# An attention and expert kernel: its attention loop with all five engines in the written order, routing in pieces, and weight casts on GpSimd

## The chip, the core and the metric

The kernel runs on one core of a Trainium2 chip. A core has five engines with a queue of instructions each: TensorE (PE, matrix products), VectorE (DVE), ScalarE (ACT), GpSimd (POOL) and SyncE (SP, which here issues DMAs). They wait for one another through semaphores. The metric is the device time of one execution in microseconds (us), and lower is better.

## The reference

Eight batches of twelve heads go through a sigmoid attention; the result is the input of a layer of eight experts, of which each token takes one. Cut to what matters:

```
scores = (q @ k^T) / sqrt(64) - log(448)          # 8 batches, 12 heads, 448 x 448
x      = (1 / (1 + exp(-scores))) @ v              # as 3584 tokens x 768
logits = normalise(x) @ normalise(expert_emb).T / tau
expert = argmax(logits);  gate = softmax(logits)[expert]
out[token] = gate * (relu(x @ w1[expert]) @ w2[expert])   # w1 768x1024, w2 1024x768
```

Weights, q and k are float32. The kernel makes of each a high half in 16 bits and a low half (value minus high half) in 16 bits, so that three products of 16-bit halves stand for one in float32.

## The kernel before, in words

**The attention loop** runs over 48 pairs of heads. In a pair TensorE makes three blocks of scores (`scores(i, 0..2)`, L364), and the fourth, shorter one for the next pair (`scores_tail(i + 1)`, L377); it turns the packed q and k of pair i + 2 (`turn`, L334) and multiplies the sigmoids with v (`av`, L392). ScalarE makes the sigmoids (L366, and L379 for the tail). `split` makes the halves of q and k out of what was turned: on VectorE for the first head (L344, L345), on ScalarE and VectorE for the second (L342, L345). `evac` brings the result of `av` out of PSUM: the high half on ScalarE (L406) and the low half on VectorE (L408). GpSimd packs q and k of pair i + 3 (`pack`, L323).

**The buffers that tie the engines together.** The pool `ps_s` has three PSUM tiles, and a pair takes four: three blocks of scores and the result of `av`. So the third block of pair i + 1 goes where the result of pair i lay, and has to wait for its `evac`. The pool `ps_t` has one tile: what is turned for pair i + 2 and the scores' tail of pair i + 1 use it in turn, so the tail waits for the `split`.

**Work beside it.** Six pairs make a batch, and two batches a group of 896 tokens. In the pairs behind a batch `chunk` computes router products (L415, summed on VectorE at L417) and `rows` turns the tokens' rows by DMA, stores them (L429, L432) and adds and squares them for the norm (GpSimd L436, ScalarE L442). Behind each of the first three groups, `route1` picks each token's expert (VectorE, L461 to L468), and `route2` counts with TensorE (L475, L476) and works out each token's place (L480 to L488, of which the last is seven comparisons into the tile POH). `select`, `early1` and `early2` do the same for an expert and two blocks of tokens that start early. From pair 30 on the weights of that expert and of the next come in by SyncE (`fetch`, L168), one piece of 128 rows in a pair, into four staging tiles; VectorE casts the high half (`high_v`, L176) and the low half (`low`, L180).

**What sets the order.** In the loop SyncE and TensorE run in the order in which the code is written (`tc.manual_schedule`). For ScalarE, VectorE and GpSimd a scheduler places the instructions by its own model of time; `tc.issue_after` sets a lower limit for a few of them. The routing's steps stand in a pair behind `scores_tail` and ahead of `evac`. Behind the loop come the rest of the router, then the experts' two layers, block of tokens by block of tokens.

## Time and profile before

| | us |
|---|---|
| median of 3 runs (892.04 to 898.67) | 892.21 |
| the profiled execution | 892.36 |
| its span, from the first instruction to the last | 890.6 |
| TensorE busy in the span | 808.4 |
| VectorE, ScalarE, GpSimd busy | 395.7, 392.8, 216.8 |
| the attention loop, first score product to last product with v | 14.4 to 360.4 |

The profile gives each group of instructions by line, engine and operation, with busy time, mean duration and the idle time of the engine ahead of it. A wait is put down to the instruction that ended it. L numbers are lines of the kernel before; the listing of the changed kernel has lines of its own (L345 there is L350, L408 is L411, L468 is L470, L364 is L367, L377 is L380, L392 is L395).

### The profile page before, as it was taken

What the parts mean: (1) busy time and instruction counts of PE and PEld (TensorE: products, weight loads), DVE (VectorE), ACT (ScalarE), POOL (GpSimd) and SP (SyncE); (2) the same over time, 40 slices, a digit from 0 to 9 for tenths busy, and PEclk for the clock granted to TensorE, in tenths of its full rate; (3) what the DMA queues carried; (4) which work ended last, traced back from release to release, by engine and by line L of the source; (5) the groups of instructions that cost most, each with busy time, mean ns of one, the idle gap of its engine ahead of it and who ended that gap; (6) DMA issues with size and microseconds to landing.
All of it is one profiled execution on the core that took longest, in us unless ns stands there. A gap on an engine that the chain in (4) does not pass through costs nothing. (4 is left out here: it accounts for less than half of the span.)

```text
span 890.6 us, 17187 instructions
## 1 busy us (share of the span) xinstructions
PE 808.4 (91%) x5720; PEld 395.0 (44%) x5720; DVE 395.7 (44%) x727; ACT 392.8 (44%) x610; POOL 216.8 (24%) x260
## 2 busy tenths in 40 slices
PE   5999989998998789898859999799999999999794
PEld 2444434343434343354425555345555555555452
DVE  4444454355577663776234115742521012434740
ACT  5667676765675666133233114542421012424540
POOL 2122333242233240113202122122121213130211
PEclk9999999999999999999969999989999999999988
DMA  5665767482989594767999569999997549779973
GB/s 145 172 151 158 170 178 168 140 216 81 244 264 263 159 227 133 169 134 198 205 198 230 135 122 288 286 250 233 294 154 127 126 104 245 217 158 275 276 215 46
DMA packets 252601, 168.13 MB, mean 189 GB/s; under 512 B 192412, under 2 KB 229766, under 8 KB 252464
## 3 DMA queue, kind: packets, MB, share of 16 engines
q1 hardware_dynamic: 242272, 131.13, 63.4%
q0 software_dynamic: 9200, 35.03, 13.4%
q8 instruction: 69, 1.13, 0.5%
q14 instruction: 68, 0.56, 0.2%
q10 hardware_dynamic: 992, 0.29, 0.1%
HBM read 103.02 MB, written 23.99 MB: 143 GB/s over the span
## 5 line engine op out<-in xcount | busy, mean ns | idle before, releaser
L219 PE MATMUL pss<-w,xt 128*128 128x512 f16 x900 | 198.5, 379 | 2.1 <-DVE hr L252 1.1
L231 PEld LDWEIGHTS <-hT 128*128 128x128 f16 x1296 | 129.5, 101 | 123.6 <-SPq L915 16.2
L231 PE MATMUL pss<-w,hT 128*128 128x384 f16 x768 | 138.1, 343 | 28.3 <-SPq L915 15.3
L366 ACT ACTIVATE att<-pss,bias_s 128x896 f32<-128x896 f32 x144 | 135.5, 1012 | 3.9 <-PE pss L364 2.9
L219 PEld LDWEIGHTS <-xt 128*128 128x128 f16 x900 | 87.5, 98 | 106.9 <-issue 4.4
L392 PE MATMUL pss<-att,vt 128*64 128x448 f32 x576 | 125.3, 560 | 8.5 <-ACT att L366 4.3
L954 POOL DMA_INDIRECT out<-ob,six x64 | 70.0, 1094 | 210.9 <-ACTq L915 124.1
L250 ACT ACTIVATE hr<-pss 128x512 f16<-128x512 f32 x66 | 37.0, 595 | 180.9 <-PE pss L219 127.0
L364 PE MATMUL pss<-kq 64*128 64x448 f16 x864 | 101.4, 356 | 12.1 <-DVE xT L408 7.2
L252 DVE SCALAR_TENSOR_TENSOR hr<-pss,hr 128x512 f16<-128x512 f32 x66 | 43.5, 687 | 150.8 <-ACT hr L250 143.3
L231 PE MATMUL pso<-w,hT 128*128 128x384 f16 x528 | 87.6, 326 | 0.0
L180 DVE SCALAR_TENSOR_TENSOR w<-stage_w,w 128x768 f16<-128x768 f32 (+1 forms) x78 | 75.9, 1002 | 22.0 <-ACT w L172 19.7
L345 DVE SCALAR_TENSOR_TENSOR kq<-ptr,kq 128x512 f16<-128x512 f32 x96 | 63.0, 657 | 45.5 <-ACT kq L342 43.8
L172 ACT ACTIVATE w<-stage_w 128x768 f16<-128x768 f32 (+1 forms) x78 | 66.5, 877 | 34.2 <-DMA stage_w<-in_moe_w 28.3
L323 POOL COPY pk<-qk 128x384 f32<-128x384 f32 x94 | 48.9, 547 | 122.3 <-issue 83.6
L924 POOL DMA_INDIRECT xg<-xs,gix x31 | 33.1, 1066 | 182.9 <-DMA xt<-xg 141.5
L392 PEld LDWEIGHTS pss<-att,vt 128*64 128x64 f32 x576 | 34.5, 136 | 80.7 <-ACT att L366 51.5
L180 DVE SCALAR_TENSOR_TENSOR w<-stage,w 128x1024 f16<-128x1024 f32 (+1 forms) x48 | 57.8, 1229 | 15.5 <-ACT w L172 14.9
L364 PEld LDWEIGHTS <-kq 64*128 64x128 f16 x864 | 38.9, 95 | 47.2 <-issue 16.5
L408 DVE SCALAR_TENSOR_TENSOR xT<-pss,xT 128x384 f16<-128x384 f32 x96 | 33.0, 384 | 53.2 <-ACT xT L406 27.0
L379 ACT ACTIVATE att_t<-ptr,bias_s 128x448 f32<-128x448 f32 x47 | 29.8, 634 | 55.6 <-PE ptr L377 42.1
L436 POOL TENSOR_TENSOR xf<-xrow 128x768 f32<-128x768 f16 x24 | 39.5, 1644 | 21.2 <-ACT xq L442 18.8
(197 smaller groups left out, 640.4 us busy)
## 6 DMA issues: line engine op xcount, KB each, us to landing
stage_w<-in_moe_w SPq DMA_DIRECT2D x64, 384.0 KB, 4.7
stage<-in_moe_w SPq DMA_DIRECT2D x40, 512.0 KB, 4.8
qk<-in_q SPq DMA_DIRECT2D x48, 192.0 KB, 3.8
qk<-in_k SPq DMA_DIRECT2D x48, 192.0 KB, 3.6
vt<-in_v SPq DMA_DIRECT2D x48, 192.0 KB, 3.4
xs<-xrow POOLq DMA_DIRECT2D x24, 384.0 KB, 4.1
stage_w<-in_moe_w SPq DMA_DIRECT2D x14, 512.0 KB, 4.5
stage<-in_moe_w SPq DMA_DIRECT2D x8, 384.0 KB, 4.2
```

The source lines that it names most:

```text
L172: nc.scalar.activation(wts[st][i][:, c, :], s, AF.Copy, scale=SW)
L180: nc.vector.scalar_tensor_tensor(wts[st][i + 1][:, c, :], s, SW, wts[st][i][:, c, :], op0=ALU.mult, op1=ALU.subtract)
L219: nc.tensor.matmul(ph[half][:, t % 2], xt[:, xi, kc, :], wts[st][wi][:, kc, half * HF:(half + 1) * HF], start=(n == 0), stop=(n == len(L1_ ...
L231: nc.tensor.matmul(po[d][:, :HD], hs[fc // 4][:, i, fc % 4, :], wts[st][wi][:, fc, d * HD:(d + 1) * HD], start=(n == 0), stop=(n == len(L2 ...
L252: d = nc.vector.scalar_tensor_tensor(hr[:, 1], ps, 0.0, hr[:, 0], op0=ALU.max, op1=ALU.subtract)
L323: en.tensor_copy(t.rearrange("p c h d -> p h c d"), qk[i][:, j])
L345: last_split[0] = nc.vector.scalar_tensor_tensor(lo[:, :n, h], x, SQK, hi[:, :n, h], op0=ALU.mult, op1=ALU.subtract)
L364: nc.tensor.matmul(ps[:, h, :S], x[r, ki, c * P:(c + 1) * P], x[r, qi, QC], start=(n == 0), stop=(n == 2))
L366: sig[0] = nc.scalar.activation(a, ps[:, :, :S], AF.Sigmoid, bias=bias_s, scale=1.0 / (8.0 * SQK * SQK))
L392: nc.tensor.matmul(pav[i][h * D:(h + 1) * D, :S], w, m, start=(c == 0), stop=(c == CM))
L436: nrm[1].tensor_tensor(xf, xr[:, 0], xr[:, 1], op=ALU.add)
L954: ins = mark[ET.Pool] = nc.gpsimd.indirect_dma_start(out.rearrange("n (h d) -> (n h) d", h=2), bass.IndirectOffsetOnAxis(ap=six[:, d, c:c ...
```

## The change

- In the loop ScalarE, VectorE and GpSimd are under the written order too, and the code of a pair is put in a new sequence: loads, `pack` of pair i + 3, scores 0 and 1, turning of pair i + 2, scores 2, `split`, squares, stores and adds of rows, turning of rows, routing pieces, low weight casts of the pair before, high weight cast and fetch of the next piece, `av`, the tasks behind a batch, `evac`, and last the tail of the scores.
- In a pair that has a square, `split` has both its high halves on VectorE (`busy`).
- `route1` runs a pair later, from the list `fill`, in the pair whose `route2` stands behind `av`; the rest of `route2` (new function `ranks`), of `select` (`choose`) and of `early1` (`early_tokens`) runs a pair later.
- High weight casts are on GpSimd, and the low cast of a piece comes a pair after its high cast. Two pieces at most are under way instead of four.

```diff
         def high_v():
             for c, s in zip(chunks, tiles):
-                nc.vector.tensor_scalar(wts[st][i][:, c, :], s, SW, None, op0=ALU.mult)
+                nc.gpsimd.tensor_scalar(wts[st][i][:, c, :], s, SW, None, op0=ALU.mult)
...
-        return ((ET.SP, fetch), (ET.DVE, high_v) if vec else (ET.Activation, high), (ET.DVE, low))
+        return ((ET.SP, fetch), (ET.Pool, high_v) if vec else (ET.Activation, high), (ET.DVE, low))
...
-        def split(ps, i):
+        def split(ps, i, busy=False):
...
-                if h:
+                if h and not busy:
                     nc.scalar.activation(hi[:, :n, h], x, AF.Copy, scale=SQK)
                 else:
                     nc.vector.tensor_scalar(hi[:, :n, h], x, SQK, None, op0=ALU.mult)
...
                 xq = nrm[0].tile([P, DM], mybir.dt.bfloat16, name="xq")
-                with tc.issue_after(sig[0].ins):
-                    nc.scalar.activation(xq, xf, AF.Square, accum_out=N2[:, g * JG + j:g * JG + j + 1])
+                nc.scalar.activation(xq, xf, AF.Square, accum_out=N2[:, g * JG + j:g * JG + j + 1])
...
             nc.vector.tensor_reduce(RK[:, sl], t2, axis=AX.X, op=ALU.add)
+
+            def rest():
+                ranks(g)
+
+            if g < NG - 1:
+                fill.append(rest)
+            else:
+                rest()
+            return pst[:, JG * E:JG * E + E]
+
+        def ranks(g):
+            j0 = g * JG
+            sl = slice(j0, j0 + JG)
             if g > GE:
                 member(sl, JG)
...
-            r = [[lambda: chunk(g, 3, 4)], [lambda: chunk(g, 5, 6)],
-                 [lambda: route1(g)], [lambda: route2(g)]]
+            r = [[lambda: chunk(g, 3, 4)], [lambda: chunk(g, 5, 6), lambda: fill.append(lambda: route1(g))],
+                 [lambda: route2(g)]]
...
-        with tc.manual_schedule(engines={ET.SP, ET.PE}):
+        lows = []
+        with tc.manual_schedule(engines={ET.SP, ET.PE, ET.Activation, ET.DVE, ET.Pool}):
             for i in range(NPAIR):
...
-                now[0] = i
-                if i in lag:
-                    lag.pop(i)()
-                if rowq:
-                    rows(*rowq.pop(0))
+                if i + 3 < NPAIR:
+                    pack(i + 3, 1)
+                    pack(i + 3, 0)
+                sq, norms[:] = norms[:], []
                 scores(i, 0)
                 scores(i, 1)
                 if i + 2 < NPAIR:
-                    turns(i + 2)
-                task()
+                    ps = ps_t.tile([P, 2, 512], F32, tag="tr", name="ptr")
+                    for j in (1, 0):
+                        turn(ps, i + 2, j)
                 scores(i, 2)
-                task()
+                if i + 2 < NPAIR:
+                    split(ps, i + 2, bool(sq))
+                for f in sq:
+                    f()
+                old, lag[:] = lag[:], []
+                for f in old:
+                    f()
+                if rowq:
+                    rows(*rowq.pop(0))
+                fs, fill[:] = fill[:], []
+                for f in fs:
+                    f()
+                for f in lows:
+                    f()
+                lows[:] = []
+                if er:
+                    if wp and (wts[1][0] is not None or wp[0][0] == 0):
+                        _, hi, lo = wp.pop(0)[1]
+                        hi[1]()
+                        lows.append(lo[1])
+                    if wq and len(wp) < 2:
+                        fetch_next()
                 for c in range(CM + 1):
                     av(i, c)
-                if i + 1 < NPAIR:
-                    scores_tail(i + 1)
...
                 evac(i)
-                if i + 3 < NPAIR:
-                    pack(i + 3, 1)
-                    pack(i + 3, 0)
-                task()
+                if i + 1 < NPAIR:
+                    scores_tail(i + 1)
```

Three places show what this does to the order of the instructions. First VectorE where the first group is routed: in the kernel before, pair 15 and the start of pair 16 (kq is the split of q and k, t, RK, KT, PM and POH belong to `route2`, xT is the `evac`):

```order
L344 TENSOR_SCALAR kq<-ptr 128x8x64
L345 SCALAR_TENSOR_TENSOR kq<-ptr,kq 128x8x64
L345 SCALAR_TENSOR_TENSOR kq<-ptr,kq 128x7x64
L480 TENSOR_TENSOR t_1631<-pss,OH 128x56
L481 TENSOR_REDUCE RK<-t_1631 128x7
L575 TENSOR_SCALAR KT<-RK 128x7
L576 TENSOR_SCALAR KT<-KT 128x7
L486 SCALAR_TENSOR_TENSOR PM<-KT,RK 128x7
L488 TENSOR_SCALAR POH<-iota_82,PM 128x128 x7
L408 SCALAR_TENSOR_TENSOR xT<-pss,xT 128x3x128
L408 SCALAR_TENSOR_TENSOR xT<-pss,xT 128x64
```

And now, pair 14, from behind its `split` on (L, MX, t, m, OH and CUM belong to `route1`):

```order
L463 TENSOR_SCALAR L<-L,rtau 128x56
L464 TENSOR_REDUCE MX<-L 128x7
L465 TENSOR_TENSOR t_1516<-L,MX 128x56
L466 TENSOR_TENSOR t_1516<-t_1516,cst 128x56
L467 TENSOR_REDUCE m_1517<-t_1516 128x7
L468 TENSOR_TENSOR OH<-t_1516,m_1517 128x56
L470 TENSOR_TENSOR CUM<-CUM,OH 128x8 x7
L482 TENSOR_TENSOR t_1542<-pss,OH 128x56
L483 TENSOR_REDUCE RK<-t_1542 128x7
L411 SCALAR_TENSOR_TENSOR xT<-pss,xT 128x3x128
L411 SCALAR_TENSOR_TENSOR xT<-pss,xT 128x64
```

The seven comparisons into POH no longer stand between two halves of `route2` and an `evac`; they come in the next pair, behind its `split`. All of `route1` now stands between the `split` and the part of `route2` that reads TensorE's counts, within one pair.

Second, TensorE at the same routing: before, at the end of pair 15 (ptr<-kq is the tail of the scores, OH and CUM are what `route1` wrote, the last row begins pair 16):

```order
L377 LDWEIGHTS kq
L377 MATMUL ptr<-kq 128x448
L475 LDWEIGHTS upper_80
L475 MATMUL pss<-OH,upper_80 128x56
L476 LDWEIGHTS ones_81
L476 MATMUL pss<-CUM,ones_81 128x56
L364 LDWEIGHTS kq
L364 MATMUL pss<-kq 128x448
```

Now, at the end of pair 14:

```order
L395 MATMUL pss<-att,vt 64x448 x6
L395 MATMUL pss<-att_t,tv_129 64x448 x2
L477 LDWEIGHTS upper_80
L477 MATMUL pss<-OH,upper_80 128x56
L478 LDWEIGHTS ones_81
L478 MATMUL pss<-CUM,ones_81 128x56
L380 LDWEIGHTS kq
L380 MATMUL ptr<-kq 128x448
```

The two products of `route2` stand ahead of the tail of the scores, in the same pair in which VectorE makes OH and CUM.

Third, VectorE in a pair with a weight cast (w_0_73 is the high half, w_1_74 the low half, L417 belongs to a `chunk`); before:

```order
L176 TENSOR_SCALAR w_0_73<-stage 128x1024
L180 SCALAR_TENSOR_TENSOR w_1_74<-stage,w_0_73 128x1024
L344 TENSOR_SCALAR kq<-ptr 128x8x64
L345 SCALAR_TENSOR_TENSOR kq<-ptr,kq 128x8x64
L345 SCALAR_TENSOR_TENSOR kq<-ptr,kq 128x7x64
L417 TENSOR_REDUCE L<-pss 128x16
L408 SCALAR_TENSOR_TENSOR xT<-pss,xT 128x3x128
L408 SCALAR_TENSOR_TENSOR xT<-pss,xT 128x64
```

Now:

```order
L349 TENSOR_SCALAR kq<-ptr 128x8x64
L350 SCALAR_TENSOR_TENSOR kq<-ptr,kq 128x8x64
L349 TENSOR_SCALAR kq<-ptr 128x7x64
L350 SCALAR_TENSOR_TENSOR kq<-ptr,kq 128x7x64
L180 SCALAR_TENSOR_TENSOR w_1_74<-stage,w_0_73 128x1024
L411 SCALAR_TENSOR_TENSOR xT<-pss,xT 128x3x128
L411 SCALAR_TENSOR_TENSOR xT<-pss,xT 128x64
```

The cast no longer stands ahead of the `split`, its high half has left VectorE, and in this pair, which has a square, the `split` has four instructions there instead of three.

More of the change, by code (lines that the diff above doesn't have):

```diff
@@ L446, in first @@
                 xf = add()
-                lag[now[0] + 1] = lambda: square(xf)
+                norms.append(lambda: square(xf))
             if now[0] < NPAIR:
-                lag[now[0] + 1] = first if now[0] + 1 not in lag else (lambda f=lag[now[0] + 1]: (f(), first()))
+                lag.append(first)
             else:
@@ L663, in attn_moe_kernel @@
                 if i == 0:
[L664 to L670 removed]
+                    expert_prep()
         now[0] = NPAIR
         ended.append(1)
[L673 to L676 removed]
+        for fs in (lag, norms, lows):
+            for f in fs:
+                f()
         while len(wp) > 1 or wq:
```

41 lines of the change are left out of this document (17 added, 24 removed).

## The prediction

> **What bounds the kernel now.** I read the page first. Its head and its row of the granted TensorE clock, in tenths over 40 slices of the span:
>
> ```profile
> span 890.6 us, 17187 instructions
> PEclk9999999999999999999969999989999999999988
> ```
>
> The profiled execution took 892.36 us, 1.8 more than its span, and the median of the runs is 892.21, so a sum against the profiled time is one against the median too. Then the stages. In each row stand the stretch, its length, the busy time of PE, PEld, DVE, ACT and POOL, the granted clock, the DMAs' share and GB/s. The first two rows are the attention loop's quieter and its heavier half; the third is a plain pair, the next five are pairs 9, 28, 38, 43 and 44, the last is what follows the loop:
>
> ```profile
> 14.43:190.10 175.67, 168.06 (x1519) 72.84 (x1516) 80.18 (x174) 122.74 (x202) 50.43 (x77) 1.00 0.64 161
> 190.10:360.40 170.30, 149.42 (x1279) 63.98 (x1277) 103.58 (x223) 107.42 (x181) 51.67 (x66) 0.98 0.74 193
> 47.50:53.63 6.13, 6.13 (x53) 2.65 (x53) 2.69 (x5) 4.45 (x8) 0.96 (x2) 1.00 0.49 132
> 73.78:80.89 7.11, 6.30 (x54) 2.63 (x52) 3.08 (x6) 5.39 (x11) 2.52 (x3) 1.00 0.57 176
> 204.66:215.24 10.58, 8.08 (x56) 3.27 (x53) 6.57 (x18) 5.25 (x10) 2.52 (x3) 0.84 0.04 13
> 278.63:288.31 9.68, 6.95 (x61) 2.94 (x60) 9.36 (x26) 5.09 (x10) 4.89 (x7) 1.00 0.97 276
> 320.23:328.63 8.40, 6.44 (x64) 2.97 (x61) 5.95 (x8) 4.16 (x8) 4.27 (x4) 1.00 1.18 218
> 328.63:337.25 8.62, 8.62 (x74) 4.15 (x73) 4.38 (x9) 5.17 (x9) 1.66 (x4) 0.80 1.12 327
> 360.40:470.00 109.60, 88.96 (x589) 46.76 (x588) 61.23 (x146) 30.68 (x47) 23.67 (x25) 0.91 0.91 191
> ```
>
> TensorE bounds the loop: a plain pair is 6.13 us, all of it TensorE. What the change can win there is TensorE's idle time, 7.6 us in the first half and 20.9 in the second, and the time in which its clock is halved. A clock of 0.84 over 10.58 us and of 0.80 over 8.62 us loses 0.16 x 10.58 + 0.20 x 8.62 = 3.4 us. So some 32 us of 892 are the most that the loop can give. Who ends the idle time, in the loop (total us, times, longest):
>
> ```profile
> PE ptr L377 <- DVE kq L345: 7.7, 9, 2.0
> PE pss L364 <- DVE xT L408: 7.2, 8, 1.5
> PE pss L364 <- ACT att L366: 4.9, 4, 1.3
> PE pss L392 <- ACT att L366: 4.3, 15, 0.7
> PE pss L392 <- DVE xT L408: 4.0, 3, 1.5
> ```
>
> These make 28.1 of the 28.5. The plain pair in order of time (start, us) tells how much room each engine has:
>
> ```profile
> 47.50 1.31 PE L364 MATMUL pss<-kq 64*128 64x448 f16 x12
> 47.58 0.69 DVE L408 SCALAR_TENSOR_TENSOR xT<-pss,xT 128x384 f16<-128x384 f32 x2 [1.37 <-PE ptr L377]
> 49.08 0.79 PE L364 MATMUL pss<-kq 64*128 64x448 f16 x6
> 49.34 0.69 DVE L344 TENSOR_SCALAR kq<-ptr 128x512 f16<-128x512 f32 x1 [1.07 <-PE ptr L334]
> 51.03 0.55 ACT L342 ACTIVATE kq<-ptr 128x448 f16<-128x448 f32 x1
> 51.62 0.62 DVE L345 SCALAR_TENSOR_TENSOR kq<-ptr,kq 128x448 f16<-128x448 f32 x1 [0.86 <-ACT kq L342]
> 52.10 0.92 PE L392 MATMUL pss<-att_t,tv 128*64 128x448 f32 x4
> 52.96 0.74 PE L377 MATMUL ptr<-kq 128*128 128x448 f16 x3
> 53.10 0.60 ACT L406 ACTIVATE xT<-pss 128x384 f16<-128x384 f32 x2 [1.52 <-PE pss L392]
> ```
>
> Call the pair's start 0. The split runs from 1.84 to 4.74 and the tail needs it at 5.46: 0.7 us of room. The low half of the pair before's evac ends at 0.77 and the third block of scores wants its tile at 1.58: 0.8 us. VectorE is free from 4.74 to 6.2.
>
> **Part by part. The written order.** (a) The 7.7 us are a split that is late, by weight casts ahead of it on VectorE or, once, by the preparation of the expert table. The split now comes first; the one left is the preparation, which stands ahead of pair 1's split. I leave 1.9 for it, nearly the longest of the nine, since all of it is now ahead of that split, and take 5.8. (b) The 7.2 us are a late evac. In pair 9 (7.11 less 6.30: 0.8 us) nothing but a square adds to the plain pair; it stood ahead of the evac on ScalarE. It is now behind the sigmoids of the pair itself, where ScalarE has room (4.45 of 6.13 busy): the split's 0.55 leaves ScalarE for VectorE in such pairs, which then splits without a gap, 0.69 + 0.69 + 0.69 + 0.62 = 2.7 us, done at about 4.5. The other causes are casts and routing pieces ahead of the evac. A low cast (1.2 us, by a row below) begins at 4.5 to 4.7, so it is done at about 6.0, when evac's low half begins: it fits. A routing piece of the length of route1 (2.87, below) does not quite: 4.5 + 2.87 + 0.69 = 8.1 against 6.13 + 1.58 = 7.7, so evac is 0.4 late, and with a cast behind it more; I leave 2.5 and take 4.7. (c) The 4.9 us are four waits for a first sigmoid that stood behind a late tail and a square; the order now forbids that: 4.9. (d) Of the 4.3 us most are waits of 0.2 for the last sigmoid, which the order does not touch: 0.8. (e) The 4.0 us are the comparisons into POH ahead of the evac; they now follow a split, with some 3 us until evac would be late; I leave 0.8 and take 3.2. Sum 19.4 us, of which (c) and most of (a) follow from the order alone.
>
> **The new wait.** route2's products on TensorE now wait in the pair in which route1 runs. Behind the loop the same chain stands undisturbed:
>
> ```profile
> 370.09 0.25 DVE L461 TENSOR_SCALAR L<-L,rtau 128x56 f32<-128x56 f32 x1
> 371.62 1.34 DVE L468 TENSOR_TENSOR CUM<-CUM,OH 128x8 f16<-128x8 f16 x7
> 372.81 0.19 PE L476 MATMUL psr<-CUM,ones 128*128 128x56 f16 x1 [0.97 <-DVE CUM L468]
> ```
>
> From L461's start to CUM's end are 2.87 us. Behind a split that ends at 4.74 this gives 7.6 to 7.7, and TensorE is through with av at 5.5: it stands 2.2 to 2.4 us, and queued behind it are the tail and all of the next pair. Pairs 14, 26 and 38 do this. In pair 38 GpSimd can hold VectorE up. Two rows tell how such a hold looks, a low cast over an addition on GpSimd:
>
> ```profile
> 322.25 2.80 DVE L180 SCALAR_TENSOR_TENSOR w<-stage,w 128x768 f16<-128x768 f32 x1
> 322.57 1.66 POOL L436 TENSOR_TENSOR xf<-xrow 128x768 f32<-128x768 f16 x1
> ```
>
> This cast of 768 elements takes 2.80 us with the addition; four of 1024 without take 4.62 together, in a row below. The Trainium skill says why, in "GPSIMD Engine Reference", section "Specifications": GpSimd's way into SBUF is shared with VectorE and contended by instructions with two SBUF inputs; these rows agree. route1's additions have two SBUF inputs, and a high cast now stands on GpSimd there, so I add 1.1 for pair 38: 2.4 + 2.4 + 3.5 = 8.3 us lost.
>
> **The halved clock.** In pair 28 TensorE waits twice before its clock falls:
>
> ```profile
> 207.10 0.74 PE L364 MATMUL pss<-kq 64*128 64x448 f16 x6 [1.21 <-ACT att L366]
> 209.13 4.17 PE L392 MATMUL pss<-att,vt 128*64 128x448 f32 x12 [1.29 <-DVE xT L408]
> ```
>
> The two lie within 3.3 us, and what the pair loses by its clock, 1.7 us, is 3.4 at half speed. Pair 44 loses as much after the 2.0 (8.40 less 6.44) that pair 43 waits. Pair 38, with waits of up to 1.5, kept its clock. Three waits of 2.3 or more should bring one to three such stretches; I take two, as many as now, so nothing won and nothing lost. The Trainium skill ("TensorE: Matmul & The Clock Gate", section "HAM oscillation — how this bites in real kernels") sets the limit at idle gaps of over about 3.4 us. The trace speaks against that here: no wait in the loop was longer than 2.0. By the page the sum would be 3.4 us lower.
>
> **Behind the loop** VectorE's chain to the last group's routing is:
>
> ```profile
> 361.64 1.88 DVE L176 TENSOR_SCALAR w<-stage 128x1024 f16<-128x1024 f32 x3
> 364.04 0.68 DVE L176 TENSOR_SCALAR w<-stage 128x1024 f16<-128x1024 f32 x1
> 364.64 4.62 DVE L180 SCALAR_TENSOR_TENSOR w<-stage,w 128x1024 f16<-128x1024 f32 x4
> 369.78 0.28 DVE L417 TENSOR_REDUCE L<-psr 128x16 f32<-128x32 f32 x2
> ```
>
> 1.88 + 0.68 = 2.6 us of high casts leave it; GpSimd can do them earlier, while the last pair runs. TensorE waits there for OH, but it also has other products and DMAs to wait for: between 0 and 2.6, I take 1.5. The experts' layers (109.6 us at a clock of 0.91 and the rest) keep their instructions and start earlier.
>
> **The casts on GpSimd.** No row has this cast. The nearest rows, with the store's issue and the fetch's landing (4.8):
>
> ```profile
> L323 POOL COPY pk<-qk 128x384 f32<-128x384 f32 x94 | 48.9, 547 | 122.3 <-issue 83.6
> L436 POOL TENSOR_TENSOR xf<-xrow 128x768 f32<-128x768 f16 x24 | 39.5, 1644 | 21.2 <-ACT xq L442 18.8
> L432 POOL DMA_DIRECT2D xs<-xrow x24 | 13.7, 569 | 82.7 <-DMA xrow<-xT 82.2 <-issue 0.4
> stage<-in_moe_w SPq DMA_DIRECT2D x40, 512.0 KB, 4.8
> ```
>
> By the copy (one input, 1.42 ns an element) 1024 elements are 1.46 us, by the addition (two inputs, 2.14) 2.2; below stands VectorE's own 0.68. I take 1.46, the copy being the nearer. Behind the loop the four could so be late by up to 4 x (1.46 - 0.68) = 3.1 instead of early. A pair's list on GpSimd is then 1.1 (two copies) + 0.6 (issue of a store) + 1.64 + 1.46 = 4.8 at most, under 6.13. It can work a pair ahead, since pack waits only for the turning of pair i + 1 (at 1.8) and the fetch is issued a pair earlier and lands within 5 us; so the low cast finds its high half ready, and the delay of a pair costs nothing. The Trainium skill, "GPSIMD Engine Reference", section "Engine selection", speaks against the move (elementwise work belongs on VectorE) but puts one-input operations at about the line rate; by that the cast would be near 1 us and the sum the same.
>
> **Sum.** 892.4 - 19.4 + 8.3 - 1.5 = 879.8 us, against the median 879.6; I say 879.7.
>
> **Rivals.** (1) Little gain: the three route2 waits are each 3.5 us and each halves the clock (3 x 1.7 = 5.1, 1.7 more than now), (b) stays whole because low casts collide with additions, nothing comes behind the loop: 892.4 - 14.7 + 10.5 + 1.7 = 889.9; between this and the sum lies 885. For it: pair 38 was 9.68 us long already with VectorE busy for 9.36. Against: GpSimd has mostly done its list when the low cast begins. (2) More: no stretch of halved clock in the loop, waits of 2.0 for route2, and the whole 2.6 behind the loop: 892.4 - 19.4 - 3.4 + 6.0 - 2.6 = 873. Against: the two stretches in the trace. The Trainium skill's rule of the clock gate, named above, would make this the case. (3) Slower: the cast on GpSimd costs 2.2 us or more and holds the port when VectorE's low cast wants it. In a pair with an addition GpSimd's cast begins at 1.8 + 1.1 + 0.6 + 1.64 = 5.1, the low cast behind it ends at 5.1 + 2.2 + 1.2 = 8.5 instead of 7.0 (7.7 less evac's 0.69), the latest that does no harm; that is 1.5 us of TensorE in the 8 of 14 pairs with casts that have an addition, 12 us, with half-clock stretches in half of them 7 more, and behind the loop 4 x 1.5 = 6 in place of the gain of 1.5. 879.8 + 12 + 7 + 7.5 = 906. It decides against the change from a cast of about 1.9 us on, and below 1.0 does no harm at all. Against: the copy's row. That the new order is not what runs is ruled out by the listings.
>
> **Chances and range.** Forecast, 874 to 884: 0.47. Little gain, 884 to 893: 0.27. More, below 874: 0.16. Slower, above 893: 0.10, of which 0.07 above 901. Faster by over 1% means below 883.3; a part of 0.03 of the forecast lies above it, so 0.60. Within 1%, to 901.1: 0.33. Under 1% this kernel's runs can't be told apart surely, as one of three lay 0.7% off. The range that leaves out 0.2 is 868 to 893: it cuts the better half of (2), down to which TensorE would have to lose nearly all of its 28 us, and all of (3).
>
> **What would show it.** TensorE's waits for evac and split (L408, L345, now L411, L350) in the loop fall to some 5 us in all, and a new row has TensorE waiting for CUM three times, over 2 us each. TensorE's idle time in the loop falls from 28.5 to about 17, the loop's end from 360.4 to about 349. The cast on GpSimd reads 1.3 to 1.6 us, and the low cast mostly 1.2. I am wrong if low casts read 2.5 us in most pairs, if TensorE doesn't stop at route2, or if the loop ends earlier and the time behind it grows by as much.

## The result, and the profile after

The changed kernel takes 865.85 us (median of 4 runs, 863.29 to 867.39) beside 893.98 for the kernel before on the same chip: a ratio of 0.9675, with a 95% interval of 0.9627 to 0.9723. It is faster, as forecast, but by more than twice the forecast: 879.7 with a range of 868 to 893. Run again in two later sets beside the kernel before, its ratio was 0.9714 (0.9654 to 0.9773) and 0.9757 (0.9701 to 0.9812). The forecast's ratio, 879.7 / 892.21 = 0.986, lies above all three intervals. Some executions of a kernel are clearly slower than its others, and all medians, ratios and intervals here leave them out.

The profiled execution took 866.07 us, 26.3 less than the one before, and its span is 864.3 us. Two windows split the span into the attention loop and what follows it (columns as in the prediction: stretch, length, busy time of PE, PEld, DVE, ACT and POOL, clock, DMA share, GB/s). The kernel before:

```profile
12.40:360.40 348.00, 319.51 (x2801) 137.30 (x2801) 185.06 (x400) 231.41 (x383) 103.55 (x145) 0.99 0.69 177
360.40:890.60 530.20, 485.57 (x2890) 255.42 (x2888) 207.28 (x320) 157.01 (x221) 109.78 (x103) 0.96 0.84 197
```

The changed kernel:

```profile
11.90:339.20 327.30, 311.86 (x2801) 136.82 (x2801) 190.58 (x406) 222.14 (x360) 149.22 (x164) 0.99 0.71 188
339.20:864.30 525.10, 482.48 (x2892) 254.44 (x2890) 205.55 (x316) 156.89 (x221) 115.25 (x105) 0.97 0.81 199
```

The loop is 20.7 us shorter. TensorE's idle time in it fell from 348.0 - 319.5 = 28.5 to 327.3 - 311.9 = 15.4, so 13.1 of the 20.7 are waits that went. The other 7.6 us came off TensorE's **busy** time, with the same 2801 products in it; 1.7 of these are the clock, which is halved for 3.4 us in this loop and was for 6.8 before. Behind the loop 5.1 us are gone in this pair of profiles. What TensorE still waits for in the loop, by the same view of waits as in the prediction:

```profile
PE ptr L339 <- ACT att_t L382: 5.2, 3, 3.0
PE pss L478 <- DVE CUM L470: 3.0, 3, 1.0
PE pss L477 <- DVE OH L468: 2.8, 3, 1.5
PE pss L367 <- DVE xT L411: 2.7, 3, 1.4
PE ptr L380 <- DVE kq L350: 1.6, 1, 1.6
```

The second and third row are the forecast wait of `route2`'s products, 5.8 us together. The waits for a late split (7.7) and a late evac (7.2 and 4.0) are down to 1.6 and 2.7. The first row is new and was not forecast.

### The profile page after: what moved, and what is told of

It is laid out like the page before. It is cut to its first block, busy times and chain, and to the rows that moved or that the text cites. A ratio compares the mean times of both kernels' runs of the same rounds, so it can differ in the third digit from the quotient of the medians.

```text
span 864.3 us, 17222 instructions
## 1 busy us (share of the span) xinstructions
PE 797.7 (92%) x5720; PEld 393.5 (46%) x5720; DVE 399.5 (46%) x729; ACT 383.4 (44%) x588; POOL 267.9 (31%) x280
## 5 line engine op out<-in xcount | busy, mean ns | idle before, releaser
L395 PE MATMUL pss<-att,vt 128*64 128x448 f32 x576 | 119.5, 548 | 0.2
L328 POOL COPY pk<-qk 128x384 f32<-128x384 f32 x94 | 45.0, 506 | 154.5 <-issue 113.1
L180 DVE SCALAR_TENSOR_TENSOR w<-stage_w,w 128x768 f16<-128x768 f32 (+1 forms) x78 | 75.9, 1003 | 18.9 <-ACT w L172 17.3
L409 ACT ACTIVATE xT<-pss 128x384 f16<-128x384 f32 x96 | 29.0, 354 | 94.5 <-DVE L L420 39.5
L180 DVE SCALAR_TENSOR_TENSOR w<-stage,w 128x1024 f16<-128x1024 f32 (+1 forms) x48 | 60.3, 1278 | 16.3 <-ACT w L172 13.7
L349 DVE TENSOR_SCALAR kq<-ptr 128x512 f16<-128x512 f32 (+1 forms) x70 | 46.6, 665 | 42.9 <-PE ptr L339 42.9
L395 PEld LDWEIGHTS pss<-att,vt 128*64 128x64 f32 x576 | 36.5, 135 | 64.3 <-ACT att L369 39.1
L367 PEld LDWEIGHTS <-kq 64*128 64x128 f16 x864 | 41.7, 96 | 42.6 <-issue 19.8
```

What stands on the lines that cost most here:

```text
L180: nc.vector.scalar_tensor_tensor(wts[st][i + 1][:, c, :], s, SW, wts[st][i][:, c, :], op0=ALU.mult, op1=ALU.subtract)
L328: en.tensor_copy(t.rearrange("p c h d -> p h c d"), qk[i][:, j])
L349: nc.vector.tensor_scalar(hi[:, :n, h], x, SQK, None, op0=ALU.mult)
L367: nc.tensor.matmul(ps[:, h, :S], x[r, ki, c * P:(c + 1) * P], x[r, qi, QC], start=(n == 0), stop=(n == 2))
L395: nc.tensor.matmul(pav[i][h * D:(h + 1) * D, :S], w, m, start=(c == 0), stop=(c == CM))
```

## The experiments

All kernels do the whole computation. "Loop" is the time from TensorE's first score product to its last product with v, read from the trace of each run (it begins at 12.4 us in the kernel before, not at the 14.4 of the table ahead, and ends at 360.4), and idle is its length less TensorE's busy time in it. Each ratio is to the kernel before, run beside it on the same chip; its interval is at 95%.

| kernel | median us | ratio (interval) | loop | idle in it | behind it |
|---|---|---|---|---|---|
| before | 893.98 | 1 | 348.0 | 28.5 | 530.2 |
| changed | 865.85 | 0.9675 (0.9627-0.9723) | 327.4 | 15.4 | 525.1 |
| old_seq_written | 932.36 | 1.0494 (1.0422-1.0566) | 385.4 | 55.5 | 528.9 |
| new_seq_scheduled | 912.84 | 1.0263 (1.0164-1.0361) | 368.9 | 40.3 | 530.9 |
| act_written | 873.62 | 0.9751 (0.9685-0.9818) | 333.4 | 19.8 | 529.2 |
| vector_written | 922.39 | 1.0296 (1.0204-1.0388) | 381.9 | 50.5 | 532.5 |
| squares_first | 885.27 | 0.9881 (0.9790-0.9972) | 338.5 | 18.7 | 538.2 |
| high_on_vector | 867.19 | 0.9756 (0.9690-0.9823) | 328.0 | 16.2 | 524.6 |
| route2_later | 864.41 | 0.9689 (0.9589-0.9788) | 320.2 | 10.8 | 529.9 |
| later_evac_first | 901.67 | 1.0086 (1.0043-1.0128) | 358.5 | 43.2 | 524.5 |
| no_busy | 874.52 | 0.9739 (0.9663-0.9815) | 334.3 | 19.1 | 526.0 |
| lows_behind | 877.77 | 0.9784 (0.9727-0.9841) | 325.7 | 14.3 | 537.7 |
| later_and_behind | 876.40 | 0.9776 (0.9711-0.9841) | 322.1 | 10.2 | 539.2 |
| after_again | 872.96 | 0.9714 (0.9654-0.9773) | 329.9 | 16.1 | 531.8 |
| before_again | 890.91 | 0.9987 (0.9924-1.0050) | 351.6 | 29.6 | 526.8 |
| after_third | 870.18 | 0.9757 (0.9701-0.9812) | 329.9 | 15.9 | 526.7 |
| tail_kept | 863.17 | 0.9675 (0.9611-0.9739) | 318.5 | 9.2 | 526.1 |

Medians are compared only where kernels ran on one chip. The kernel before took 889.76 us there beside old_seq_written, new_seq_scheduled, high_on_vector and route2_later, 894.98 beside act_written, vector_written, squares_first and later_evac_first, 897.29 beside no_busy, lows_behind, later_and_behind and after_again, and 892.10 beside before_again, after_third and tail_kept. Loops are compared across chips too, each from one profile: the changed kernel's own three are 327.4, 329.9 and 329.9 us, so a difference of 2.5 in the loop says nothing.

### The sequence or the order

The change does two things to the loop: it writes the code in a new sequence, and it puts ScalarE, VectorE and GpSimd under the written order. First the old code, with its order frozen as written (some limits on early starts fall away in the loop, as the written order leaves them no use):

```diff
+    loop = [0]
...
-            with tc.issue_after((after or mark)[en].ins):
+            with nullcontext() if loop[0] else tc.issue_after((after or mark)[en].ins):
...
-        with tc.manual_schedule(engines={ET.SP, ET.PE}):
+        loop[0] = 1
+        with tc.manual_schedule(engines={ET.SP, ET.PE, ET.Activation, ET.DVE, ET.Pool}):
```

> The kernel before with one part of the change alone: all five engines in the written order, the code's old sequence kept (squares at a pair's start ahead of its sigmoids, evac behind the tail, routing and casts where they were, high casts on VectorE). Theory A, the gain comes from where the new sequence puts ScalarE's and VectorE's work: this has nearly none of it, 885 us or more, perhaps slower than before. Rival B, freezing the order is what counts, since the scheduler's model placed things badly: 875 or less.

Then the new code with those three engines left to the scheduler:

```diff
-        with tc.manual_schedule(engines={ET.SP, ET.PE, ET.Activation, ET.DVE, ET.Pool}):
+        with tc.manual_schedule(engines={ET.SP, ET.PE}):
```

> The changed kernel with ScalarE, VectorE and GpSimd given back to the scheduler; sequence, pieces and GpSimd casts stay. Theory A: without the frozen order squares and pieces slip ahead of sigmoids and evac again, 873 to 885. Rival B: the same range or above. Rival C, that the pieces and the casts on GpSimd carry the gain whatever the order: 868 or less.

Either part alone makes the kernel slower, by 4.9% and by 2.6%; the second lies far above the 873 to 885 us expected of it. The waits of TensorE in the run with the old sequence frozen (the longest row):

```profile
PE pss L394 <- ACT att L368: 37.1, 63, 6.9
```

And in the run with the new sequence left to the scheduler:

```profile
PE pss L395 <- ACT att L369: 18.5, 13, 6.0
PE ptr L339 <- ACT att_t L382: 9.0, 7, 3.1
```

Both stop TensorE at sigmoids, that is, at ScalarE's queue. The old sequence was written for a scheduler that moves things, and the scheduler undoes the new one. The gain is that of the two together.

### Which engine's order

```diff
-        with tc.manual_schedule(engines={ET.SP, ET.PE, ET.Activation, ET.DVE, ET.Pool}):
+        with tc.manual_schedule(engines={ET.SP, ET.PE, ET.Activation}):
```

> The changed kernel with VectorE and GpSimd given back to the scheduler, and ScalarE, TensorE and SyncE in the written order. Giving back all three made the loop 41 us longer than in the changed kernel, and TensorE's waits there named ScalarE's sigmoids most. Theory A1, ScalarE's order is what has to be frozen: the loop is back at 335 us or less, the time at 876 or less. Theory A2, VectorE's order is: the loop stays above 350, the time above 888.

```diff
-        with tc.manual_schedule(engines={ET.SP, ET.PE, ET.Activation, ET.DVE, ET.Pool}):
+        with tc.manual_schedule(engines={ET.SP, ET.PE, ET.DVE}):
```

> The counterpart: ScalarE and GpSimd given back to the scheduler, VectorE in the written order. A1: the loop stays above 350 us, the time above 888. A2: loop at 335 or less, the time 876 or less. Both above: the two orders work only together.

With ScalarE alone fixed, the loop is 333.4 us, 3.5 to 6.0 more than with all three. What is left there is mainly the late split, since the scheduler puts casts and routing ahead of it on VectorE again (the longest wait is in pair 43, where a low cast ahead of the split waits 6.24 us for GpSimd's high cast):

```profile
PE ptr L380 <- DVE kq L350: 14.5, 9, 5.0
```

With VectorE alone fixed, the loop is 381.9, worse than with neither, and the sigmoids stop TensorE for 37 us:

```profile
PE pss L395 <- ACT att L369: 19.3, 10, 4.6
PE ptr L339 <- ACT att_t L382: 17.7, 9, 3.6
```

So it is ScalarE's order that the new sequence needs most: it takes the loop from 368.9 to 333.4 us. The order of VectorE and GpSimd together is worth 3.5 to 6.0 us once ScalarE's stands, and that of VectorE alone is worth nothing without it. GpSimd's order alone was not tried. These weights are those of the new sequence; in the kernel before, the waits named VectorE for 18.9 of the 28.1 us.

### Why busy time went: late sigmoids

In pair 10 of the kernel before nothing is stopped for more than 0.2 us, and yet the pair is 0.57 longer than the plain 6.13. The window and ScalarE's and TensorE's instructions there (start, us; att is the sigmoid, xq the square):

```profile
80.89:87.59 6.70, 6.50 (x54) 2.48 (x52) 2.72 (x7) 5.19 (x10) 0.96 (x2) 1.00 0.32 88
```

```profile
81.01 0.83 ACT L442 ACTIVATE xq<-xf 128x768 bf16<-128x768 f32 x1
81.83 2.79 ACT L366 ACTIVATE att<-pss,bias_s 128x896 f32<-128x896 f32 x3
82.88 0.20 PEld L392 LDWEIGHTS pss<-att,vt 128*64 128x64 f32 x4 [0.65 <-ACT att L366]
82.89 2.77 PE L392 MATMUL pss<-att,vt 128*64 128x448 f32 x12 [0.20 <-ACT att L366]
```

The same pair in the changed kernel:

```profile
79.00:85.13 6.13, 6.13 (x54) 2.65 (x54) 3.22 (x6) 4.89 (x9) 1.01 (x3) 1.00 0.34 97
```

```profile
79.84 2.81 ACT L369 ACTIVATE att<-pss,bias_s 128x896 f32<-128x896 f32 x3
81.29 2.48 PE L395 MATMUL pss<-att,vt 128*64 128x448 f32 x12
82.53 0.85 ACT L444 ACTIVATE xq<-xf 128x768 bf16<-128x768 f32 x1
```

The square stood ahead of the three sigmoids and now stands behind them. Before, TensorE makes its products with v at the pace at which ScalarE brings the sigmoids: the first one starts 0.20 late, and the twelve take 2.77 us instead of 2.48. The weight loads (PEld) show the waiting, 0.65 ahead of the first block; of it only the 0.20 reads as idle time of PE. The groups of these weight loads, before and in the changed kernel, from their pages:

```profile
L392 PEld LDWEIGHTS pss<-att,vt 128*64 128x64 f32 x576 | 34.5, 136 | 80.7 <-ACT att L366 51.5
```

```profile
L395 PEld LDWEIGHTS pss<-att,vt 128*64 128x64 f32 x576 | 36.5, 135 | 64.3 <-ACT att L369 39.1
```

They are a sign of the waiting and not its size, since 39.1 us are left in the changed kernel, where TensorE's idle time ahead of these products is 0.2 (their row stands below). To test the square's place, the squares go back ahead of the sigmoids and all else stays as changed:

```diff
                 sq, norms[:] = norms[:], []
+                for f in sq:
+                    f()
...
-                for f in sq:
-                    f()
```

> The changed kernel with a pair's squares written at its start, ahead of its sigmoids, everything else in place; 24 squares of 0.83 to 1.0 us. Theory H, TensorE's busy time hides waits (late sigmoids stretch its products instead of showing as idle time): the loop grows by 8 to 24 us and at least half of it shows as busy time, the total 873 to 888. Rival I, what is lost shows as idle time: the loop grows and its busy time stays within 2 us of 312. Rival J, the place of the squares costs nothing: 868 or less.

The loop is 11.1 us longer (338.5), of which 3.3 are idle time and 7.8 are busy time; 1.7 of the 7.8 are one more stretch of halved clock. Pairs 10, 11, 17, 22 and 23, which have a square and nothing else that is late, take 6.70 us each before, 6.13 in the changed kernel, and 6.70 again here. The row of waits in that run, pair 10's products with v, and the group of all such products in its loop:

```profile
PE pss L395 <- ACT att L369: 5.9, 22, 0.7
```

```profile
81.81 2.77 PE L395 MATMUL pss<-att,vt 128*64 128x448 f32 x12 [0.21 <-ACT att L369]
```

```profile
L395 PE MATMUL pss<-att,vt 128*64 128x448 f32 x576 | 126.6, 560 | 6.0 <-ACT att L369 5.9
```

The same group of 576 products before and in the changed kernel, from their pages:

```profile
L392 PE MATMUL pss<-att,vt 128*64 128x448 f32 x576 | 125.3, 560 | 8.5 <-ACT att L366 4.3
```

```profile
L395 PE MATMUL pss<-att,vt 128*64 128x448 f32 x576 | 119.5, 548 | 0.2
```

The square's place alone gives the products with v their old 125 to 127 us back. So the busy time that went is, for the most part, waiting that read as work. The squares' place is worth 8.6 to 11.1 us of the loop by this run, against the changed kernel's three loops. A part of the difference in busy time is the halved clock, of which each stretch adds 1.7 us. Without it 5.9 of the 7.6 us are left. In a second pair of profiles, shown further down, each loop has three such stretches; there the busy time differs by 8.1 us and the group of products with v by 5.2 (126.7 and 121.5).

The Trainium skill says in "Perfetto Trace Analysis", section "Identifying the Most-Contended Engine", that the busy time of matrix products is no good measure of how close a kernel is to what the engine can do, as pipelined instructions look smaller in the trace. These rows agree with the rule and show another reason: the same products look longer, 125.3 against 119.5 us, where their inputs come late.

### The casts on GpSimd

```diff
-                nc.gpsimd.tensor_scalar(wts[st][i][:, c, :], s, SW, None, op0=ALU.mult)
+                nc.vector.tensor_scalar(wts[st][i][:, c, :], s, SW, None, op0=ALU.mult)
...
-        return ((ET.SP, fetch), (ET.Pool, high_v) if vec else (ET.Activation, high), (ET.DVE, low))
+        return ((ET.SP, fetch), (ET.DVE, high_v) if vec else (ET.Activation, high), (ET.DVE, low))
```

> The changed kernel with the high casts back on VectorE, ahead of nothing but av's evac, low casts still a pair later. Theory A: VectorE was busy for 4 to 5 of 6.1 us in the pairs with casts, so 0.6 more costs little there; some 1 to 2 us behind the loop: 866 to 870. Rival C: relief of VectorE by GpSimd is a main part: 874 or more.

Putting the high casts back on VectorE changes nothing that shows: a loop of 328.0 against 327.4 us, and 524.6 behind it against 525.1. Yet the cast's price was far off. Two groups of the changed kernel:

```profile
L176 POOL TENSOR_SCALAR w<-stage 128x1024 f16<-128x1024 f32 x12 | 34.1, 2847 | 5.2 <-DMA stage<-in_moe_w 5.2
L176 POOL TENSOR_SCALAR w<-stage 128x768 f16<-128x768 f32 x8 | 18.8, 2346 | 0.0
```

A cast of 128x1024 takes 2.85 us on average, above the 2.2 that the prediction gave as its upper end, and 0.80 on VectorE in high_on_vector. In the sum it does no harm. GpSimd had room for it, and what it holds up on VectorE at one place comes back at another: in high_on_vector pair 38 waits 0.8 less at `route2` and pair 40 0.25 less, but pairs 39 and 44 wait 0.9 and 1.2 us that they don't wait in the changed kernel.

### The wait of route2

In the changed kernel `route2`'s products wait in the pair in which `route1` runs. Here they come a pair later, and with them all that stands behind them in the list:

```diff
-                 [lambda: route2(g)]]
+                 [], [lambda: route2(g)]]
```

> The changed kernel with an empty slot ahead of route2, so that TensorE's counts come a pair after route1. If TensorE's three waits at route2 cost what they show (5.8 us, and a stretch of halved clock of 1.7 behind the third): 858 to 861. If the time comes back elsewhere, as a late evac or by the weights starting a pair later: 865 or more.

The two rows of 3.0 and 2.8 us are gone, no stretch of halved clock is left in the loop, and the loop is 320.2 us, 7.2 to 9.7 less. The time behind it is 4.8 more in this profile, and the ratio (0.9689) can't be told from the changed kernel's (0.9675), so the 858 to 861 us expected were missed; whether those 4.8 come from this edit, later runs put in doubt. The next kernel has the later `route2` too, and `evac` ahead of the tasks behind a batch:

```diff
-                r += [[select]]
+                r[-1] += [select]
...
-                r += [[early1]]
+                r[-1] += [early1]
...
+                evac(i)
                 if soon and i + 1 < NPAIR:
...
-                evac(i)
```

> The changed kernel with route2 a pair later (with select and early1 in the same slot, so that the weights don't start later) and with evac written ahead of the tasks behind a batch, so that ScalarE's half of it waits for no product read by VectorE. If TensorE's waits at route2 (5.8 us) and for the tail's sigmoid (5.2) go without a successor: loop 315 us or less, 853 to 860. If evac ahead of the tasks only moves the wait: 860 to 866.

This was meant to free the evac from the routing. It took 901.67 us beside 894.98 for the kernel before, so it lost all of the gain, which neither expectation foresaw. Its longest row of waits:

```profile
PE pss L418 <- DVE xT L411: 27.3, 18, 2.1
```

The products of `chunk` (L418) go into the PSUM tile that `evac` reads, so they now wait for the evac: about 1.5 us in each of 18 pairs. The tasks stand ahead of the evac for a reason.

### The split of pairs with a square

```diff
-                    split(ps, i + 2, bool(sq))
+                    split(ps, i + 2, False)
```

> One part of the change undone: in the 24 pairs with a square, the second head's high half of the split stays on ScalarE (0.55 us each). The prediction's step (ScalarE has room in such a pair: 5.0 of 6.13 us busy, 5.55 with it): the loop stays within 1 us of 327.4, 864 to 868 in all. Rival (a late square pushes the evac's high half and the tail's sigmoid back as the written evac of another run did): 0.3 to 0.4 us in each of the 24 pairs, partly as idle time for the evac's low half (L411) or the tail (L382) and partly as longer av products, the loop 7 to 10 us longer, 872 to 877.

On the chip of this run the changed kernel's loop was 329.9 us and this one's 334.3, of which 3.0 are idle time and the rest is covered by one more stretch of halved clock (1.7); it lies between the two expectations. Quiet pairs with a square (9 to 11, 17, 21 to 23) keep their 6.13, so ScalarE has the room there, as the prediction's count of its work said. Pairs 16 and 29, which have routing as well, stand idle for 1.05 and 1.50 us instead of 0.23 and 1.06. Most of the rest is in pair 33, which waits 2.4 here, and 0.8, 1.5 and 2.3 in three profiles of the changed kernel itself. The medians, 874.52 and 872.96, don't differ surely: `busy` is worth about 1 us that can be named.

### The new wait, and the low casts

The three waits of the first row (5.2 us) are in pairs 28, 33 and 40 (1.42, 0.77 and 3.02). Pair 40, on VectorE, ScalarE, GpSimd and TensorE, in order of time:

```profile
279.06 1.63 POOL L439 TENSOR_TENSOR xf<-xrow 128x768 f32<-128x768 f16 x1 [1.79 <-ACT xq L444]
279.07 1.65 DVE L501 SCALAR_TENSOR_TENSOR PM<-KT,RK 128x7 f32<-128x7 f32 x1
280.67 2.13 POOL L176 TENSOR_SCALAR w<-stage 128x768 f16<-128x768 f32 x1
280.75 2.17 DVE L503 TENSOR_SCALAR POH<-iota,PM 128x128 f16<-128x128 f16 x7
282.83 0.94 DVE L180 SCALAR_TENSOR_TENSOR w<-stage,w 128x768 f16<-128x768 f32 x1
283.69 0.15 DVE L547 TENSOR_TENSOR ec<-pss,eoh 128x8 f32<-128x8 f32 x1
283.88 0.61 ACT L409 ACTIVATE xT<-pss 128x384 f16<-128x384 f32 x2 [4.91 <-DVE ec L547]
284.37 0.64 ACT L382 ACTIVATE att_t<-ptr,bias_s 128x448 f32<-128x448 f32 x1
285.15 0.40 PE L339 MATMUL ptr<-ident,pk 64*128 64x64 f32 x6 [3.02 <-ACT att_t L382]
```

A small product of `early1` lies in spare columns of the PSUM tile with the pair's result, and ScalarE's half of the evac waits until VectorE has read it (ec). VectorE comes late to that: comparisons and a low cast stand ahead, and it is held by GpSimd. Behind it on ScalarE's queue stands the tail's sigmoid, and behind that on TensorE the next pair's turning, since both use the one tile of `ps_t`. In pair 28 the small product is that of `select`, in pair 33 that of a `chunk`, read behind a low cast of 2.46 us. Undisturbed, behind the loop, the two routing steps take this:

```profile
352.04 0.17 DVE L501 SCALAR_TENSOR_TENSOR PM<-KT,RK 128x7 f32<-128x7 f32 x1
352.24 1.23 DVE L503 TENSOR_SCALAR POH<-iota,PM 128x128 f16<-128x128 f16 x7
```

So 1.65 - 0.17 + 2.17 - 1.23 = 2.4 us of pair 40's delay are those two instructions beside GpSimd's. The run high_on_vector bears this out for the second: with no cast on GpSimd, the comparisons of pair 40 take 1.23 us. One edit takes the cast out of the way, to behind the evac:

```diff
-                for f in lows:
-                    f()
-                lows[:] = []
+                ls, lows[:] = lows[:], []
...
                 evac(i)
+                for f in ls:
+                    f()
```

> One edit against the changed kernel: the low casts on VectorE stand behind the evac instead of ahead of it. Theory (the new waits for ScalarE's tail sigmoid are the evac's two halves pushed back by what stands ahead of them on VectorE, of which the cast is a part): the wait of 0.77 goes in pair 33, and pairs 40 and 41 lose 0.95 less each, so the loop is 2.7 us shorter (about 324.7), 861 to 865 in all. Rival (VectorE has no better place for the cast: from the low half of evac at 0.77 to the split at 1.84 there are 1.07 us, and a cast takes 0.95 to 2.05): the split is late by up to 0.3 beyond its room in 14 pairs, TensorE waits for L350 by up to 4 us, the loop stays or grows, 866 to 870.

And with it the later `route2`, its followers in the same pair:

```diff
-                 [lambda: route2(g)]]
+                 [], [lambda: route2(g)]]
...
-                r += [[select]]
+                r[-1] += [select]
...
-                r += [[early1]]
+                r[-1] += [early1]
```

> Two edits against the changed kernel: the counting of tokens (the first part of route2) one pair behind route1, with what follows it in the batch's list in the same pair, and the low casts behind the evac. Theory (the waits in the loop are separate and add up): as with the later counting alone 7.2 us less loop, and 2 to 3 less by the casts, loop 317 to 319, and 857 to 860 in all if the time behind the loop stays at 525. Rival (the later counting pushes routing and weights out of the loop, 4.8 us behind it as in the run with the later counting alone): loop 317 to 319, but 530 behind it, 861 to 865.

The changed kernel ran beside them once more:

> The changed kernel once more, unchanged, to see how much of the loop and of the time behind it repeats. If both are properties of the program: TensorE's loop 327.4 us with 15.4 idle, 525 us behind it, 864 to 867 in all. If the time behind the loop (524.5 to 538 among the kernels so far, with 31 to 49 us of halved clock) is a matter of the execution, the loop repeats within 0.5 us and what follows it differs by 2 us or more.

The changed kernel did not repeat within 0.5 us: its loop is 329.9 here and was 327.4, and what follows it 531.8 instead of 525.1. In the loop both edits gained on it, to 325.7 and 322.1 us, of which 1.7 each are one stretch of halved clock less. But the medians went the other way, 872.96, then 877.77 and 876.40. All of the gain, and more, was given back behind the loop (531.8, then 537.7 and 539.2). Neither expectation had this for the first edit; for both together the rival had 530. The place of it in the run lows_behind, on SyncE, VectorE and TensorE:

```profile
339.31 8.74 SPq L427 DMA_TRANSPOSE xrow<-xT  x4
348.31 0.86 SPq L168 DMA_DIRECT2D stage<-in_moe_w  x1
358.07 1.22 DVE L180 SCALAR_TENSOR_TENSOR w<-stage,w 128x1024 f16<-128x1024 f32 x1 [12.85 <-POOL w L176]
361.68 0.23 PE L477 MATMUL psr<-OH,upper 128*128 128x56 f16 x1 [12.36 <-DVE OH L468]
```

The last fetch of a weight piece came behind the four transposes of the last batch on SyncE. A low cast on VectorE waited 12.9 us for the high cast of its piece, the last group's routing stood behind that cast, and TensorE waited 12.4 us for OH. The order of SyncE's instructions is different there: the changed kernel issues that fetch ahead of the transposes. With the low casts ahead of the evac again in the last pairs, that order comes back:

```diff
                 ls, lows[:] = lows[:], []
+                if i > 43:
+                    for f in ls:
+                        f()
+                    ls = []
```

> As the run with later counting and casts behind the evac, but from pair 44 on the low casts stand ahead of the evac again, so that SyncE has the last fetch of a weight piece ahead of the last batch's four transposes. Theory (the time given back was that fetch: TensorE's wait of 12.4 us for OH, as VectorE's routing stood behind a cast whose piece had not come): that wait is gone, loop 322 to 324, behind it 525 to 532 as in the changed kernel, 6 to 8 us faster than the changed kernel on this chip (ratio to before 0.962 to 0.966). Rival (something else behind the loop doesn't begin earlier, whatever the loop does): loop 322 to 324, behind it 537 or more, no faster than the changed kernel.

### Does the change win time behind the loop?

The kernel before and the changed one ran unchanged beside tail_kept, each with a profile:

> The kernel before once more, unchanged, with a profile on the same chip as the next two. If the change wins time behind the loop: 530 us or more behind it here, and at least 4 less in the repeat of the changed kernel. If what was seen there is the execution's own spread (half-clock stretches behind waits for DMAs): a difference under 3 us, of either sign. Loop 348 in both cases.

> The changed kernel once more on the same chip. Loop 327 to 330 with 15.4 to 16.1 idle. Behind it 525 to 532: with the change winning there, 4 us or more below the kernel before in the run beside it; with spread alone, within 3 us of it.

The windows of the loop and of what follows it, first the kernel before:

```profile
11.90:363.50 351.60, 321.98 (x2801) 138.31 (x2801) 186.44 (x400) 231.67 (x382) 104.60 (x145) 0.99 0.69 175
363.50:890.30 526.80, 482.63 (x2890) 254.31 (x2888) 206.78 (x320) 156.56 (x221) 106.79 (x103) 0.97 0.84 198
```

The changed kernel:

```profile
11.90:341.70 329.80, 313.93 (x2801) 137.43 (x2801) 191.52 (x406) 222.25 (x360) 150.23 (x165) 0.98 0.70 187
341.70:868.40 526.70, 482.09 (x2892) 254.14 (x2890) 205.13 (x316) 157.43 (x221) 111.60 (x104) 0.97 0.83 198
```

And tail_kept:

```profile
11.90:330.40 318.50, 309.27 (x2801) 135.71 (x2801) 187.97 (x406) 223.15 (x360) 146.26 (x163) 1.00 0.74 192
330.40:856.50 526.10, 481.14 (x2892) 253.82 (x2890) 206.01 (x316) 157.07 (x221) 115.20 (x106) 0.97 0.83 199
```

Behind the loop the three take 526.8, 526.7 and 526.1 us: on this chip the change wins nothing there. The 5.1 us of the first two profiles lie within what the same program does from run to run, as the changed kernel's three profiles have 525.1, 531.8 and 526.7. A gain of a few us behind the loop is neither shown nor ruled out by five profiles with such a spread. In the loop the change wins 21.8 us on this chip, 13.7 of idle and 8.1 of busy time.

In tail_kept the wait of 12.4 us is gone, the loop is 11.3 us shorter than the changed kernel's, no clock is halved in it, and the gain arrives: 863.17 against 870.18 us, 7.0 less, as the theory said. The loop is 3.5 us shorter than the theory had it at the least. The ratios to the kernel before are 0.9675 (0.9611 to 0.9739) and 0.9757 (0.9701 to 0.9812). These intervals overlap, but the four runs of tail_kept (858.40 to 866.71) lie all below the four of the changed kernel on the same chip (869.03 to 871.17).

## Why the prediction was right or wrong

**The step that failed** stands in its first part: "So some 32 us of 892 are the most that the loop can give." It counted TensorE's idle time and the halved clock, took TensorE's busy time as work, and so the sum has no term for busy time. The loop gave 20.7 us, less than those 32, but 7.6 of them came from where the prediction saw nothing to win: 1.7 by the clock, and 5.9 (8.1 in the second pair of profiles) that were mostly waiting for late sigmoids, which stretches the products with v and reads as busy. The sign of it was on the page before and was not used: the weight loads of L392 with 51.5 us of idle time put down to att. By the prediction's own example, pair 9, a square "adds" 0.8 us of idle time; the pair behind it is 0.57 too long by a stretch that shows 0.2 of idle time. Part (d) touches the very thing, "waits of 0.2 for the last sigmoid, which the order does not touch", and was wrong in that: the order moved the square from ahead of the sigmoids to behind them, all 4.3 us went but 0.2 at most (0.8 forecast), and the busy time with them.

**What the miss is made of.** The sum was 879.8 us against the profiled execution of 866.1, so 13.7 were missing: 7.6 of busy time in the loop, 2.0 of idle time in it (13.1 won, 11.1 forecast), 3.6 behind it (5.1 and 1.5), and 0.5 ahead of it, as the loop begins at 11.9 instead of 12.4. The 3.6 may be chance, as the runs above show.

**The written order.** (a) was forecast to leave 1.9, measured 1.6, and it is the expert table's preparation in pair 1, as said. (b) and (e) were to leave 2.5 + 0.8 and left 2.7, now in pairs 16, 29 and 41. (c) is gone, as forecast. With (d) nearly whole, what was there before fell from 28.1 to 4.3: 23.8 where 19.4 was forecast.

**The new wait of route2** was right in mechanism and place (pairs 14, 26 and 38), and too long by 2.5 us: 5.8 instead of 8.3, with 1.66, 1.66 and 2.46. What GpSimd adds in pair 38 was 0.8, not 1.1; in high_on_vector, with no cast on GpSimd, pair 38 waits 1.68 like the others.

**What was not forecast** is the wait of 5.2 us for the tail's sigmoid, through the evac that waits for a small product's reading. It is what the prediction said to look for, a routing piece ahead of the evac, but it came out at another row. Idle time in the loop came to 15.4 us, forecast about 17; this agrees by luck, because the 5.2 made up for what (d) and route2 gave.

**The halved clock** was to stay at two stretches. The loop's profiles of the changed kernel show 3.4, 6.8 and 10.2 us of it, those before 6.8 and 10.2: no difference that repeats, as forecast. Of the three waits that should bring the stretches, the two of 1.66 us brought none, and that of pair 38 one in all three profiles.

**Behind the loop** 1.5 us were forecast, between 0 and 2.6. One pair of profiles showed 5.1, the other 0.1. The changed kernel's own spread of 6.7 is wider than either, so the runs don't settle this term.

**The casts on GpSimd** were forecast at 1.46 us between 0.68 and 2.2, and took 2.85 (128x1024) and 2.35 (128x768) on average, 2.12 to 3.74 one by one. By rival (3), which "decides against the change from a cast of about 1.9 us on", the kernel would have been slower. Its price came true and its consequence did not. GpSimd's list, which it added up in one pair, is spread over pairs; in pair 34, for one, a cast begins 0.9 us and the next 4.6 us behind the pair's start. high_on_vector shows that where these casts run is worth nothing that shows. The sentence on the low cast, "finds its high half ready", held in the loop but for its last pair, where VectorE sat idle for GpSimd's casts twice, for 2.2 us in all.

**Rival (2)**, 873 us, with a range cut at 868, is nearest to the result, but by luck: it had the route2 waits right (5.8 instead of 6.0), but the clock not, the 2.6 behind the loop stay open, and it has no term for the busy time either.

## What to carry to other kernels

Idle time is a lower bound of what an in-order engine loses: where its inputs come at the pace of another engine, the waiting hides in stretched instructions, so take the weight loads' waits as a sign of it, and compare each stage's length with that of the quietest stage of its kind. Fix the order of the engine that feeds the bottleneck first (here ScalarE), and try the order and the sequence written for it together: here either alone was worse than what was there, by 4.9% and 2.6%. When a loop's gain doesn't arrive in the total, look for one wait at its border, and give a difference of the rest of the program no cause before the same program has been profiled twice.

## What the runs showed of the hardware that was not expected

A one-input cast from float32 to 16 bits on GpSimd took 2.76 us for 128x1024 and 2.12 for 128x768 at its quickest, 2.7 to 2.8 ns an element, while its copy of 128x384 in float32 takes 1.3 ns. The Trainium skill, "GPSIMD Engine Reference", section "Engine selection", puts one-input operations at about the line rate; this cast was four times VectorE's 0.68 us, and no run here shows why.

VectorE's instruction with two SBUF inputs took 1.65 us instead of 0.17 beside GpSimd's addition, and the seven comparisons, which have one such input and a column, 2.17 instead of 1.23 beside the cast (rows of pair 40). With the cast on VectorE (high_on_vector) the comparisons took 1.23 there too, and the first instruction, still beside the addition, 1.48.

The halved clock doesn't follow from the length of one wait. Pair 38 waits for 1.47 and 0.99 us, and pair 39 behind it runs at a clock of 0.79; pair 40 waits for 3.02 us at once, and keeps the full clock in this profile. The windows of pairs 38 to 40:

```profile
264.18:273.24 9.06, 6.60 (x57) 2.85 (x58) 6.58 (x19) 4.10 (x7) 6.92 (x6) 1.00 0.91 246
273.24:281.40 8.16, 8.16 (x59) 3.63 (x57) 6.24 (x13) 4.76 (x8) 3.90 (x5) 0.79 0.74 208
281.40:290.17 8.77, 5.75 (x50) 2.22 (x46) 7.60 (x20) 5.22 (x10) 4.45 (x5) 1.00 0.43 140
```

The traces show what the two differ in. The granted clock changes only on a grid of steps of 3.41 us, and each stretch is one step or several. In the loops of the seventeen profiles 41 steps are halved behind a step at full clock; in the step just ahead of them TensorE sat idle for 1.45 us once and for 1.77 to 3.41 us in the other 40. In none of the 1575 steps at full clock that were followed by another did it sit idle for more than 1.81 us. Pair 38's two waits fall into one step (2.29 us idle). Pair 40's 3.02 us are split over two (1.40 and 1.62); in the changed kernel's other two profiles its wait is 3.18 and 3.19 us, of which one step holds most (2.52 and 2.37 us idle), and there the clock is halved behind it. So it is the idle time within one step that goes with the halving, and where a wait falls on the grid differs from run to run.
